# Attention blocks of the first 256 tokens worked by token halves, their FFN in 128-token units, and a written-out order

## The chip, the cores and the metric

The kernel runs on one core of one Trainium2 chip. A core has five engines that run at the same time and wait for each other by semaphores: TensorE (PE, matmuls into PSUM), VectorE (DVE), ScalarE (ACT), GpSimd (POOL) and SyncE (SP, which here only issues transfers). Transfers (DMA) run beside them on 16 DMA engines; they are issued from the queues of SP, ACT and POOL. Each engine takes its instructions strictly in the order in which they were recorded.

The metric is the device time of one execution in microseconds (us). Before the change it is 300.65 us, the median of three runs (299.34 to 301.24).

## What is computed

Sparse attention, followed by a gated FFN on its output, cut to what matters:

```python
B, H, S, D = 4, 8, 768, 64                       # q, k, v, float32
k_min, k_max = min and max of k over chunks of 32 tokens
ub = sum over d of max(q * k_min, q * k_max)     # a bound per query and chunk, causal by chunk
top = the 6 chunks of largest ub                 # per query
scores = q @ k.T / 8, masked to those chunks and to earlier tokens
x = softmax(scores) @ v                          # -> (3072 tokens, 512)
xn = x / sqrt(mean(x * x) + 1e-6) * rms_g
g, val = xn @ w_gate, xn @ w_val                 # 512 -> 1536
out = (g * sigmoid(g) * val) @ w_out             # 1536 -> 512, float32
```

A query in the first 192 tokens has at most 6 chunks before it, so only the last 64 queries of the first 256 tokens need the choice of chunks.

## The kernel before

**Tiling.** The work is twelve blocks of 256 tokens of one batch element, in the order `(0,0) (1,0) (2,0) (3,0) (0,1) (1,1) (0,2) (2,1) (1,2) (3,1) (2,2) (3,2)` (batch element, block). This text counts them from 0. The eight heads are two groups of four. A block's attention needs the keys and values of its own and the earlier blocks of its batch element, so the first four blocks need only themselves. The first half of the FFN, 512 to 1536, is twelve matmul groups for each block, six for gate and six for value; a group fills one PSUM bank (128 x 512).

**One block.** Loads of k, q and v (line 528); `job` transposes k and q in 32 x 32 squares on VectorE (794), casts them to bf16 (`half`, 801 on ScalarE or 802 on GpSimd), takes the minimum and maximum of each chunk (809) and prepares the bounds' operands (815 to 888). `pick` computes the bounds on TensorE (680; 698 for the first four blocks), and on VectorE the six best chunks and from them a mask (723 to 755). `unit` computes scores (922) and adds the mask by a matmul (933); exp (972), a triangle that zeroes later tokens (942, GpSimd), then `values` (998), a reciprocal (1013) and a normalization (1017). `norm` takes the mean square (1034 ScalarE, 1040 and 1042 GpSimd), scales (1052 to 1068) and turns the tokens into `xsT` (on TensorE with an eviction at 1087 or 1091 for the first four blocks, by a DMA transpose for the others). `ffn` does gate and value (1122), tanh (1129), tg (1133), a copy of the value (1141), the product hh (1144 on GpSimd, 1137 on VectorE), the projection (1169), its eviction (1184 or 1187) and the store (1191).

**The first blocks.** Blocks 0 to 2 (`PACKED`) load k and q so that eight tokens lie together in a partition. For blocks 0 and 1 (`SPLIT`) scores, exp and values are done in two parts by tokens, for each head group by itself, xsT by 128 tokens, and the first third of gate and value in groups of sixteen matmuls of 128 columns; all other groups are eight matmuls of 256 columns. For blocks 0 to 2 (`APART`) each head group has its own `pick`. Block 3 loads k and q in sixteen transfers and v in two.

**Order.** `Plan.op` records each operation with its engine or engines, reads, writes and buffers; `Plan.run` (255) then sets the order with a model of costs: it takes, time by time, the operation whose inputs and buffers are there, by a table of due times (`DUE`, 125). Where TensorE would stand idle in the first 60 us of that plan, it puts in matmuls that write nothing of use (1245): narrow ones at first, wide ones later. Two things hold back transfers. `GATES` (508) makes the weights' loads wait for the first `dk` of block 0, and `HELD` (584) makes block 2's loads wait for the second third of wg, and block 3's for the first of wo. Weights come in thirds, in the order wg0, wv0, wg1, wv1, wg2, wv2, wo0, wo1, wo2, issued from GpSimd's queue, which also does work; loads and stores are issued from SP's.

Buffers: kraw 2, qraw 3 and vraw 2 (each a whole block), pt 4, hh 13, rden 3, two pairs of PSUM banks for scores (S) and four banks for the rest (F).

Of the kernel before, what the change touches and what calls it, by code (L numbers as in the profile page):

```python
# [18 lines left out]
HUGE = 3.0e38  # L19


# [15 lines left out]
class Rings:  # L37
    FETCHED = 3.3

    def __init__(self):  # L40
        self.now = 0.0
        self.queue = {}
        self.wait = []

    def _step(self, until):
        while True:
            heads = [q[0] for q in self.queue.values() if q]
            nxt = self.wait[0][0] if self.wait else None
            if not heads:
                if nxt is None or nxt > until:  # L50
                    return
                self.now = max(self.now, nxt)
            else:
                cycle = sum(d[1] for d in heads)
                end = self.now + min(d[0] for d in heads) * cycle
                stop = min(end, until, nxt if nxt is not None else end)
                if stop > self.now:
                    for d in heads:
                        d[0] -= (stop - self.now) / cycle
                    self.now = stop  # L60
                for q in self.queue.values():
                    if q and q[0][0] <= 1e-9:
                        q[0][2](self.now)
                        q.pop(0)
            while self.wait and self.wait[0][0] <= self.now + 1e-12:
                _, ring, d = self.wait.pop(0)
                ahead = sum(x[0] * x[1] for x in self.queue.get("POOL", ()))
                if ring != "POOL" and not d[3] and ahead > 0.0 and not self.queue.get(ring):
                    d[3] = True
                    self.wait.append((self.now + min(self.FETCHED, ahead), ring, d))  # L70
                    self.wait.sort(key=lambda w: w[0])
                    continue
                self.queue.setdefault(ring, []).append(d)
            if self.now >= until and not (self.wait and self.wait[0][0] <= until):
                if not any(q and q[0][0] <= 1e-9 for q in self.queue.values()):
                    return

    def add(self, t, ring, packets, cost, op):
        self._step(min(t, self.wait[0][0]) if self.wait else t)

        def landed(now, op=op):
            op.done = now + (0.9 if op.dma[2] else 1.2) + op.slack
        op.done = None
        self.wait.append((t, ring, [packets, cost, landed, False]))
        self.wait.sort(key=lambda w: w[0])
        self.guess()

    def room(self, ring, t):

        other = Rings()  # L90
        other.now = self.now
        other.queue = {r: [list(d) for d in q] for r, q in self.queue.items()}
        other.wait = [(w, r, list(d)) for w, r, d in self.wait]
        for q in list(other.queue.values()) + [[d for w, r, d in other.wait]]:
            for d in q:
                d[2] = lambda now: None

        def held():
            return sum(d[0] for d in other.queue.get(ring, ())) + sum(
                d[0] for w, r, d in other.wait if r == ring)  # L100

        while held() > 85.0:
            t = max(t, other.now) + 0.25
            other._step(t)
        return t

    def guess(self):
        other = Rings()
        other.now = self.now
        other.queue = {r: [list(d) for d in q] for r, q in self.queue.items()}  # L110
        other.wait = [(t, r, list(d)) for t, r, d in self.wait]
        other._step(1e9)


class Plan:

    SHARES = ("qx", "scale", "relu", "bd0", "bd1", "dk", "mk")
    PATIENT = {"DVE": 0.6, "ACT": 0.6}  # L120
    STICK = 25
    RESERVED = ("hh",)
    HOP = {"PE": 0.055, "ACT": 0.04, "DVE": 0.04, "POOL": 0.075, "SP": 0.06}

    DUE = (
# [282 lines left out]
def kernel(  # L408
# [796 lines left out]
    for i in range(len(ORDER)):  # L1205
# [3 lines left out]
        if i > 1:  # L1209
            loads(i)  # L1210
# [68 lines left out]
```

## Time and profile before

| | us |
|---|---|
| median of three runs (lowest, highest) | 300.65 (299.34, 301.24) |
| span of the profiled execution, first to last instruction | 297.4 |
| busy: TensorE | 282.5 (95% of the span) |
| busy: VectorE | 217.1 (73%) |
| busy: ScalarE | 216.7 (73%) |
| busy: GpSimd | 155.6 (52%) |
| bytes moved by DMA | 35.08 MB, 118 GB/s over the span |

The span is the profiled execution's own time as far as the page gives one; the runs of the table's first line are timed around the whole program. "Busy" counts filler matmuls too. Where the engine named as a bound is busy nearly throughout, the reader looks for the stretches where it is not, and for what of its work is not needed.

### The profile page before, as it was taken

The numbers are of one execution on the slowest core, as the hardware profiler recorded it, in microseconds if no ns is written. First come the engines' busy times: TensorE is split into PE (matmuls) and PEld (weight loads), VectorE is DVE, ScalarE is ACT, GpSimd is POOL, SyncE is SP. The second block draws the span as 40 slices with busy tenths as digits, with TensorE's granted clock in tenths as the row PEclk, the third lists the DMA queues.
The fourth block names the chain that finished last, engine by engine and source line by source line (L and its number), as shares of the span: only waits on it lengthen the run. The fifth ranks groups of instructions, "written<-read, shape, count | busy, mean of one in ns | idle before, by whom it ended". The sixth has DMA issues, their size and how long they took to land.

```text
span 297.4 us, 11418 instructions
## 1 busy us (share of the span) xinstructions
PE 282.5 (95%) x4672; PEld 213.4 (72%) x4672; DVE 217.1 (73%) x623; ACT 216.7 (73%) x372; POOL 155.6 (52%) x266
## 2 busy tenths in 40 slices
PE   7879999999999996999999999899999999999994
PEld 7548777657858854878767787488688778678763
DVE  6987774977998998888999999679356454456430
ACT  4897877688979876987985797677587668565331
POOL 4885858755976864475583276538044114214120
PEclk9999999999999999999999999999999999999998
DMA  7999998755676656654768576511014021011011
GB/s 188 208 204 206 255 197 163 159 130 134 141 194 154 144 136 103 149 100 110 205 135 162 108 193 150 133 40 39 0 57 55 1 82 30 2 73 35 2 71 71
DMA packets 86388, 35.08 MB, mean 118 GB/s; under 512 B 74816, under 2 KB 81728, under 8 KB 86336
## 3 DMA queue, kind: packets, MB, share of 16 engines
q1 hardware_dynamic: 80736, 29.12, 42.6%
q0 software_dynamic: 4752, 4.72, 9.4%
q8 instruction: 36, 0.59, 0.8%
q10 hardware_dynamic: 848, 0.53, 0.7%
q14 instruction: 16, 0.13, 0.2%
HBM read 28.58 MB, written 6.29 MB: 117 GB/s over the span
## 4 chain that ended last, share of the span: by engine, by line
PE 76%; DMA 9%; DVE 4%; ACT 4%; SPq 3%; POOL 1%; issue 1%; DVEq 0%; POOLq 0%; ACTq 0%
PE F L1122 39%; PE F L1169 18%; PE S L922 6%; PE F L998 6%; PE F L680 3%; SPq L528 3%; PE S L933 2%; DMA xsT<-xs 2%; DMA qraw<-in_q_dram 2%; DMA vraw<-in_v_dram 2%; DMA kraw<-in_k_dram 2%; DVE kx L809 1%; POOL hh L1144 1%; DVE m L739 1%; ACT th L1129 1%
## 5 line engine op out<-in xcount | busy, mean ns | idle before, releaser
L972 ACT ACTIVATE pt<-S 128x1024 bf16<-128x1024 f32 (+3 forms) x104 | 85.6, 857 | 19.7 <-PE S L933 18.2
L1144 POOL TENSOR_TENSOR hh<-tg,vs 128x512 bf16<-128x512 bf16 x48 | 55.7, 1164 | 42.6 <-ACT vs L1141 22.9
L1133 DVE SCALAR_TENSOR_TENSOR tg<-th,F 128x512 bf16<-128x512 bf16 x72 | 48.4, 680 | 39.3 <-ACT th L1129 33.7
L1122 PE MATMUL F<-xsT,wg 128*128 128x256 bf16 (+1 forms) x608 | 72.6, 267 | 3.7 <-DVE xnat L1017 1.7
L1122 PE MATMUL F<-xsT,wv 128*128 128x256 bf16 (+1 forms) x608 | 72.4, 267 | 0.6 <-DMA xsT<-xs 0.3
L1169 PE MATMUL F<-wo,hh 128*128 128x512 bf16 (+1 forms) x300 | 68.5, 371 | 1.8 <-POOL hh L1144 0.6
L1122 PEld LDWEIGHTS <-wg 128*128 128x128 bf16 x608 | 55.6, 98 | 13.5 <-issue 2.7
L1122 PEld LDWEIGHTS <-wv 128*128 128x128 bf16 x608 | 55.2, 98 | 9.7 <-DMA vraw<-in_v_dram 0.8
L1129 ACT ACTIVATE th<-F 128x512 bf16<-128x512 f32 x72 | 42.5, 598 | 19.7 <-PE F L1122 17.4
L942 POOL TENSOR_SCALAR_AFFINE_SELECT pt<-pt 128x512 bf16<-128x512 bf16 x48 | 32.2, 674 | 32.3 <-ACT pt L972 31.7
L1169 PEld LDWEIGHTS <-hh 128*128 128x128 bf16 x300 | 27.7, 98 | 28.4 <-issue 1.8
L1141 ACT ACTIVATE vs<-F 128x512 bf16<-128x512 f32 x48 | 28.7, 598 | 13.2 <-PE F L1122 10.1
L922 PE MATMUL S<-qb,kb 32*128 32x256 bf16 (+1 forms) x800 | 32.8, 253 | 2.3 <-ACT qb L801 2.0
L809 DVE TENSOR_REDUCE kx<-kT 128x16 f32<-128x512 f32 x48 | 30.4, 664 | 0.0
L998 PEld LDWEIGHTS <-pt 128*128 128x128 bf16 x672 | 24.8, 98 | 3.1 <-issue 0.3
L998 PE MATMUL F<-VX,pt 128*128 128x65 bf16 x672 | 26.6, 194 | 0.2 <-ACT vs L1141 0.2
L922 PEld LDWEIGHTS <-kb 32*128 32x128 bf16 x800 | 13.9, 92 | 15.0 <-issue 14.4
L933 PE MATMUL S<-mtd,chunkrow 32*128 32x128 bf16 (+2 forms) x384 | 20.5, 203 | 0.2 <-issue 0.2
L933 PE MATMUL S<-mto,chunkrow 32*128 32x128 bf16 (+2 forms) x384 | 19.9, 203 | 0.0
L1017 DVE TENSOR_TENSOR xnat<-F,rden 128x256 bf16<-128x256 f32 x48 | 19.2, 415 | 0.7
L933 PEld LDWEIGHTS <-chunkrow 32*128 32x128 bf16 x768 | 18.5, 93 | 1.2 <-issue 0.4
L1034 ACT ACTIVATE junk<-xnat 128x512 bf16<-128x512 bf16 x24 | 15.1, 631 | 5.4 <-DVE xnat L1017 5.0
(71 smaller groups left out, 337.2 us busy)
## 6 DMA issues: line engine op xcount, KB each, us to landing
vraw<-in_v_dram SPq DMA_DIRECT2D x24, 256.0 KB, 4.4
out_dram<-osb SPq DMA_DIRECT2D x23, 256.0 KB, 2.4
kraw<-in_k_dram SPq DMA_DIRECT2D x72, 64.0 KB, 2.4
qraw<-in_q_dram SPq DMA_DIRECT2D x72, 64.0 KB, 2.2
QX<-qT SPq DMA_DIRECT2D x32, 64.0 KB, 2.7
wg<-in_moe_w_gate_dram POOLq DMA_DIRECT2D x3, 512.0 KB, 12.3
wv<-in_moe_w_val_dram POOLq DMA_DIRECT2D x3, 512.0 KB, 14.3
wo<-in_moe_w_out_dram POOLq DMA_DIRECT2D x3, 512.0 KB, 23.5
```

What stands on the lines that cost most here:

```text
L809: plan.op(f"ext{n}{J}", "DVE", 0.585, 0.67, lambda n=n, op=op: VE.tensor_reduce(out=at(kx)[:, g, n], in_=at(kT).rearrange("p h (j c x) -> ...
L922: TE.matmul(s[a // 2][:, a % 2, c0:c0 + q1 - q0], kbt[r, t, ks], qbt[r, t, q0:q1], start=(t == 0), stop=(t == 1 and not mask), skip_group_ ...
L933: TE.matmul(o, chunkrow[r, BLK * kg + P * e:BLK * kg + P * (e + 1)], mv, start=False, stop=(d == 1), skip_group_check=True)
L942: GE.affine_select(out=d, in_=d, compare_op=ALU.is_ge, fill=0.0, base=0, pattern=[[0, 4], [1, P]], channel_multiplier=-1)
L972: lambda pt=pt, hs=hs, c0=c0, c1=c1, x=sc[hp]: SE.activation(out=at(pt)[:, hs, c0:c1], in_=at(x)[:, :, c0:c1], func=ACT.Exp, scale=SCALE), ...
L998: TE.matmul(o[:, a, :], p_[:, a, off:off + P], vt[:, e, a, :], start=(kb_ == 0 and a == 0), stop=(kb_ == nkb - 1 and a == 3), skip_group_c ...
L1122: TE.matmul(at(p_)[:, n * W:(n + 1) * W], w[:, g, ht * P:(ht + 1) * P], at(xT)[:, g, x0:x0 + W], start=(g == 0), stop=(g == NP - 1), skip_ ...
L1129: plan.op(f"tanh{U}.{hp}", "ACT", 0.48, 0.6, lambda th=th, gp=gp: SE.activation(out=at(th), in_=at(gp), func=ACT.Tanh, scale=0.5), pri - 0 ...
L1133: VE.scalar_tensor_tensor(out=at(tg), in0=at(th), scalar=1.0, in1=at(gp), op0=ALU.add, op1=ALU.mult), pri - 30, reads=[th, gp], writes=[tg ...
L1141: plan.op(f"vcopy{U}.{hp}", "ACT", 0.48, 0.6, lambda vs=vs, vp=vp: SE.activation(out=at(vs), in_=at(vp), func=ACT.Copy), pri + 0.1, reads= ...
L1144: plan.op(f"hh{U}.{hp}", "POOL", 1.11, 1.16, lambda tg=tg, vs=vs, hh=hh: GE.tensor_tensor(out=at(hh), in0=at(tg), in1=at(vs), op=ALU.mult) ...
L1169: TE.matmul(at(op)[:, cs], at(key)[:, o:o + P], wo[:, ht, cs], start=(ht == 0), stop=(ht == NHT - 1), skip_group_check=True)
```

## The change

**Blocks 0 to 3** are now done by `early`, in eight units of 128 tokens, in the order (0,0) (1,0) (0,1) (1,1) (2,0) (2,1) (3,0) (3,1) (block, half). A load brings one unit's k or q of four heads, with four tokens together in a partition, in 128 KB; block 3 is loaded in this way too, with eight transfers for k and q. Buffers for raw data are halved and doubled in number (kraw 4, qraw 6, vraw 4). A unit's transpose, cast, minimum and maximum cover all eight heads. The first half needs no choice of chunks: its scores for both head groups are one operation, with two exp and two triangles of 128 x 512. The second half has one `pick` for both groups, then scores, exp and triangle for each group. Every 128 tokens have an rms, a turn and an xsT of their own.

**Their FFN** is all in groups of sixteen matmuls of 128 columns, a third of gate or value at a time. **Later blocks** do what they did; layouts of kx, BD and VX are changed to suit.

**The order** is no longer planned: `SEQUENCE` lists the operations, `SLOTS` the buffers, `CHOICE` the engine where there are several, `WARM` the fillers (46 narrow, 35 wide; before 77 and 39). `HELD` is empty; `GATES` names the first transpose of k. Where the weights' issues now stand in GpSimd's queue: wg0 and wv0 after the first two triangles; wg1 and wv1 with thirteen operations ahead of them after those; wg2 behind the first hh; wv2 after the next rms; wo0 after the fifth hh, wo1 after the next rms, wo2 after one hh more. The recorded operations number 1553, before 1580, without fillers.

```diff
+SEQUENCE = [
+    3, 34, 35, 36, 37, 25, 19, 13, 6, 21, 23, 33, 29, 44, 0, 30, 7, 17, 16, 1, 22, 18, 14, 39, 26, 27, 40, 45,
...
+WARM = [
+    (42, 46, 0, 0), (63, 8, 0, 1), (89, 11, 2, 1), (102, 5, 0, 1), (111, 2, 1, 1), (119, 4, 2, 1), (181, 2, 2,
+    1), (310, 3, 2, 1)]
...
-    def run(self, in_order=(), fill=None):
+    def run(self, fill):
...
+        self.slot = dict(zip(keys, SLOTS))
...
+        for place, x in enumerate(SEQUENCE):
...
-    buffers("kraw", 2, [P, NG, 8, 2, CH], FP32)
-    buffers("qraw", 3, [P, NG, 8, 2, CH], FP32)
-    buffers("vraw", 2, [P, 2, NG, 4, D], FP32)
+    buffers("kraw", 4, [P, 512], FP32)
+    buffers("qraw", 6, [P, 512], FP32)
+    buffers("vraw", 4, [P, NG, 4, D], FP32)
...
-    buffers("rden", 3, [P, 4], FP32)
+    buffers("rden", 8, [P, 4], FP32)
...
-    GATES = {"0": "dk(0, 0, 0)", "1": "dk(0, 0, 0)", "2": "dk(0, 0, 0)", "o": "dk(0, 0, 0)"}
-    SPLIT = {0, 1}
-    APART = {0, 1, 2}
+    GATES = {x: "turn k(0, 0)" for x in "012o"}
+    EARLY = {0, 1, 2, 3}
+    UNITS = [(0, 0), (1, 0), (0, 1), (1, 1), (2, 0), (2, 1), (3, 0), (3, 1)]
...
-    HELD = {2: (("wg", 1), ("wg", 1)), 3: (("wo", 0), ("wo", 1))}
+    HELD = {}
...
+    def load_early(i, nm, src, x):
+        b, m = ORDER[i]
+        key = (nm + "raw", b, m, x)
+        sv = src[b].rearrange("(g a) (m x r j) d -> g m x a r (j d)", a=4, m=NBLK, x=2, r=32)
+        for g in range(NG):
+            dma(f"load {nm}{b}{m}{x}{g}", ("SP", "ACT")[g] if (i, x) == (0, 0) else "SP", sv[g, m, x],
+                lambda g=g: at(key)[:, 256 * g:256 * (g + 1)], 8, 0.051, -500 + 10 * i + x, writes=[key],
+                takes=() if g else [(key, nm + "raw")], behind=() if g else HELD.get((i, x), ()))
...
+    def early(i):
...
+                def half(eng, T=T, hb=hb):
+                    o, t = flat(hb).rearrange("p (y r j) -> p y j r", j=4, r=32), quads(flat(T))
...
+        prepare(0)
...
+        def first():
+            for g in range(NG):
+                product([at(x)[:, :, P * g:P * (g + 1)] for x in sc], kcols(b, 0, g, 0), qcols(0, g), False)
...
+        yield
+        prepare(1)
...
+        pick(i, tuple(range(NG)))
...
+            def second(g=g, sc=sc):
+                for e in range(2):
+                    s = [at(x)[:, :, P * e:P * (e + 1)] for x in sc]
+                    product(s, kcols(b, 0, g, e), qcols(1, g), True)
+                    forbid(s, mtd, mto, g, P * e, slice(0, 1))
...
-    def ffn(i):
-        cut = NHT // 3 if i in SPLIT else 0
-        pieces = [((s,), h) for s in whole for h in range(0, cut, 4)] + [
-            (whole, h) for h in range(cut, NHT, 2)]
+    def ffn(i, pieces):
...
+    units = {i: early(i) for i in sorted(EARLY)}
+    for i, x in UNITS:
+        next(units[i], None)
+        norm(i, (x,), due_attn(i) + (7 if x else -3))
...
+    thirds = range(0, NHT, NHT // 3)
+    for h in thirds:
+        for i, x in UNITS[:4]:
+            ffn(i, [((x,), h)])
+    for i, x in UNITS[:4]:
+        project_out(i, (x,))
+    for i, x in UNITS[4:]:
+        ffn(i, [((x,), h) for h in thirds])
+        project_out(i, (x,))
+    for i in range(len(ORDER)):
+        if i not in EARLY:
+            ffn(i, [((0, 1), h) for h in range(0, NHT, 2)])
+            project_out(i, (0, 1))
```

The order of the first operations of TensorE after the change: scores of unit (0, 0), of (1, 0), values of both, turn (0, 0), pick 0, first gate group of (0, 0), turn (1, 0), pick 1, first second-half scores of block 0, first gate group of (1, 0), and from there FFN groups of blocks 0 and 1 with the second halves' attention between them; the first projection follows after the last of the 24 groups of blocks 0 and 1.

More of the change, by code (lines that the diff above doesn't have):

```diff
@@ L34, in __init__ @@
         self.alts = {eng: (occ, lat, fn)}
[L37 to L112, printed above, removed]
@@ L392, in run @@
             for key in o.uses:
[L393 removed]
                 left[key] -= 1
                 if not left[key]:
[L396 removed]
+                    held[self.pool_of[key], self.slot[key]] = None
+            gone.add(x)
             order.append(o)
[L398 to L401 removed]
         self.order = order
[L403 removed]
@@ new lines, in job @@
+            o = plan.op(f"scores{J}{kg}", "PE", pe, pe + 0.2, unit, pri,
+                        reads=keys(b, kg, g) + [qb, mtd, mto, mtd + (g,), mto + (g,), "chunkrow"],
+                        writes=sc + [pt], takes=[(x, "S") for x in sc] + [(pt, "pt")])
+            o.mode = "row"
+            for hp in range(2):
+                hs = slice(2 * hp, 2 * hp + 2)
+                plan.op(f"exp{J}{kg}{hp}", "ACT", occ, lat, lambda pt=pt, hs=hs, c1=c1, x=sc[hp]: SE.activation(
+                    out=at(pt)[:, hs, 0:c1], in_=at(x)[:, :, 0:c1], func=ACT.Exp, scale=SCALE), pri,
+                    reads=[sc[hp], pt], writes=[pt + (hp,)])
+                if kg == m:
+                    plan.op(f"tri{J}{hp}", "POOL", 0.595, 0.64, triangle(pt, hs, BLK, 0), pri,
+                            reads=[pt + (hp,), pt], writes=[pt + ("t", hp)])
```

737 lines of the change are left out of this document (328 added, 409 removed), and 198 rows, old and new, of tables (DUE, SEQUENCE, SLOTS).

## The prediction

> **What bounds the kernel now.** The page comes first: which engine is full, and in which slices it isn't.
>
> ```profile
> PE 282.5 (95%) x4672; PEld 213.4 (72%) x4672; DVE 217.1 (73%) x623; ACT 216.7 (73%) x372; POOL 155.6 (52%) x266
> ...
> PE   7879999999999996999999999899999999999994
> ```
>
> TensorE is the bound: 282.5 of 297.4 us, so 14.9 us idle, and the gaps lie in the first slices, in the one of 6 tenths (about 112 to 119 us) and at the end. But part of the busy time is filler. The groups kept apart by shape:
>
> ```profile
> L1245 PE MATMUL F<-chunkrow,ident 128*128 128x512 bf16 x39 | 10.2, 380 | 0.0
> ...
> L1245 PE MATMUL F<-ident 128*128 128x128 bf16 x77 | 6.4, 265 | 1.7 <-POOL eps L551 1.7
> ```
>
> Line 1245 writes nothing that is used. The small ones take 6.4 us in one run; the wide ones, at the 0.22 us a piece that ten 128x512 projections show below (2.32 us with the last drain), 8.5. Idle and filler make 29.8 us, useful matmuls some 267.6. No order can win more than those 29.8. Where they lie, the timeline of TensorE tells (start, duration, what):
>
> ```profile
> 22.85 1.07 PE L1122 MATMUL F<-xsT,wg 128*128 128x128 bf16 x16
> ...
> 41.99 1.07 PE L1122 MATMUL F<-xsT,wg 128*128 128x128 bf16 x16
> 42.89 1.06 PE L1122 MATMUL F<-xsT,wv 128*128 128x128 bf16 x16
> ...
> 49.56 2.32 PE L1169 MATMUL F<-wo,hh 128*128 128x512 bf16 x10
> ...
> 55.33 1.04 PE L1122 MATMUL F<-xsT,wg 128*128 128x256 bf16 x8
> ...
> 58.09 1.04 PE L1122 MATMUL F<-xsT,wg 128*128 128x256 bf16 x8
> 58.97 1.04 PE L1122 MATMUL F<-xsT,wv 128*128 128x256 bf16 x8
> 59.93 0.43 PE L698 MATMUL F<-qT,BO 64*64 64x32 f32 x16
> ...
> 60.65 0.42 PE L698 MATMUL F<-qraw,BO 64*64 64x32 f32 x16
> ```
>
> The reader should see that the first FFN matmul stands at 22.85 us; that before it TensorE has only the small attention of two blocks; and that the FFN of the first two blocks, 24 groups of 0.88 us (58.09 to 58.97) or 21 us, is through only at 59.85. Two thirds of the loss are start-up. The start-up waits for data. Bytes moved and shares of the DMA engines by stretch (last two columns: DMA share, GB/s):
>
> ```profile
> 0.00:5.00 5.00, 3.29 (x32) 3.29 (x33) 2.84 (x4) 1.49 (x2) 3.61 (x34) 1.00 0.61 161
> 5.00:10.00 5.00, 3.94 (x59) 3.43 (x58) 4.60 (x8) 4.08 (x5) 1.58 (x6) 1.00 1.09 224
> 10.00:15.00 5.00, 5.00 (x126) 2.89 (x124) 4.34 (x24) 4.09 (x11) 5.00 (x8) 1.00 1.09 210
> ```
>
> From 5 us on the DMA engines are full. And the weights, by tile (issue times on POOL, then time to landing):
>
> ```profile
> L528 POOL DMA_DIRECT2D wg<-in_moe_w_gate_dram x3: 767/777/992, 9.8 to 14.2; - x3
> DMA to landing us min/median/max: 7.9/12.3/17.8
> L528 POOL DMA_DIRECT2D wv<-in_moe_w_val_dram x3: 773/775/777, 10.8 to 15.0; - x3
> DMA to landing us min/median/max: 10.2/14.3/21.6
> L528 POOL DMA_DIRECT2D wo<-in_moe_w_out_dram x3: 747/762/857, 16.4 to 21.8; - x3
> DMA to landing us min/median/max: 22.6/23.5/25.2
> ```
>
> So the first third of wg lands at 17.7, of wv at 21.0, the last of wg at 32.0, of wv at 36.6, wo from 39 to 47: about 3.4 to 4.5 us apart.
>
> **The change part by part.** *FFN of the first four blocks in 128-token units.* Before, 8 groups were of sixteen 128-column matmuls; now 48 are. 41.99 to 42.89 is 0.90 us for sixteen, against 0.88 for eight of 256: forty groups more at 0.02 is 0.8 us at most, and I take 0.3. The weight loads double there (640 more); the row below gives 98 ns for one, so if none were hidden sixteen would take 1.57 us and the forty groups 27 us more. They are hidden in the two groups above, so zero is the end I take.
>
> ```profile
> L1122 PEld LDWEIGHTS <-wg 128*128 128x128 bf16 x608 | 55.6, 98 | 13.5 <-issue 2.7
> ```
>
> The Trainium skill (TensorE: Matmul & The Clock Gate, Back-to-back issue gap) speaks against this part: a sustained stream of weight load and matmul takes about 81 ns each at 128 columns, not the 56 of an isolated one. By it the 640 small matmuls that replace 320 wide ones would cost an estimated 16 us. The two groups above, at 56 ns, do not agree with it.
>
> *The first unit sooner.* Work now starts when half a block has landed, 128 tokens of all heads. Two rows show how landing follows bytes:
>
> ```profile
> 5.07 1.30 DVE L794 STREAM_TRANSPOSE kT<-kraw 128x512 f32<-128x512 f32 x2 [0.54 <-DMA kraw<-in_k_dram]
> ...
> 17.06 0.71 DVE L794 STREAM_TRANSPOSE qT<-qraw 128x512 f32<-128x512 f32 x1 [0.60 <-DMA qraw<-in_q_dram]
> ```
>
> The first 0.5 MB is usable at 5.07, and 2.6 MB (k, q, v of block 0, k, q of block 1) at 17.06, with the weights beside them from 9.8 on. In the new order of SP the first 0.5 MB are k and q of the first 128 tokens. So the first scores and values come sooner. But VectorE's queue then holds the transpose of the second half of block 1's k ahead of the reciprocals of unit (1, 0), and ScalarE's holds that unit's square ahead of the first xsT. That k is the 2.4th MB. Without the weights it would land at 13.4 (2.4 MB by the three rates, plus 1.2), with them by 17.0: I take 15, in the middle. From there, at these means:
>
> ```profile
> L809 DVE TENSOR_REDUCE kx<-kT 128x16 f32<-128x512 f32 x48 | 30.4, 664 | 0.0
> L1017 DVE TENSOR_TENSOR xnat<-F,rden 128x256 bf16<-128x256 f32 x48 | 19.2, 415 | 0.7
> L794 DVE STREAM_TRANSPOSE kT<-kraw 128x512 f32<-128x512 f32 x24 | 16.1, 692 | 1.2 <-DMA kraw<-in_k_dram 1.1
> ...
> L1034 ACT ACTIVATE junk<-xnat 128x512 bf16<-128x512 bf16 x24 | 15.1, 631 | 5.4 <-DVE xnat L1017 5.0
> ...
> L1087 ACT ACTIVATE xsT<-F,rmsg 128x128 bf16<-128x128 bf16 x8 | 2.3, 395 | 0.0
> ```
>
> transpose 0.7, reciprocals 0.3, one reduction 0.7, two norms 0.8, square 0.8, four xsT activations 1.2: first FFN group at 19.4, 3.4 us sooner than 22.85. The first wg is there (17.7).
>
> *Picks of both head groups at once.* Twelve of them instead of fifteen on VectorE; its rows are small and it idles in this stage. In the sum: nothing.
>
> *Weights later, and behind work.* The issues of the first third stay near 9.8. But POOL now has small work between the others: thirteen operations, two rms among them, stand ahead of the second third's two (I get 15.5 and 21 us), and ahead of the last third two triangles, two casts of k and q, a cast of v and one hh:
>
> ```profile
> L1144 POOL TENSOR_TENSOR hh<-tg,vs 128x512 bf16<-128x512 bf16 x48 | 55.7, 1164 | 42.6 <-ACT vs L1141 22.9 <-DVE tg L1133 18.7 <-DVE mtd L749 1.0
> ...
> L942 POOL TENSOR_SCALAR_AFFINE_SELECT pt<-pt 128x512 bf16<-128x512 bf16 x48 | 32.2, 674 | 32.3 <-ACT pt L972 31.7
> ```
>
> That hh needs the gate and value groups of unit (1, 0), done by my count at 26; so the last wg goes out at about 28.8 (it was 14.2). It lands 7.9 us later at the most favourable row, less if the queue is empty; I take 35.5, and wv at 39.2. Queued behind wg is the rms of unit (0, 1), whose xsT TensorE takes up at about 32: just in time.
>
> *TensorE's queue, added up.* After 19.4: the picks keep the second group to 23; four groups of the first third to 26.1; with the second third at 25.5 and 29, units (0, 0), (1, 0) and (0, 1) and the second scores to 34.7; the last third at 35.5: three gate groups to 38.2, wait to 39.2, then ten groups (8.8), a turn (0.2), one pick of matmuls (1.1, as 59.93 to 61.1) and one unit of scores (0.5): 49.9. All 24 groups are then done, with the same attention as before at 49.56, where 20 were (the last four stand at 55.33 to 59.85). Lead: 4 x 0.88 less 0.35, or 3.2 us.
>
> *What is late next.* The last wo, behind an hh of the last third on POOL, lands at about 50.4 (four weights 3.7 apart after 39.2 would say 50.3), and the first projection waits 0.5 for it. On SP the loads of block (1, 1)'s k stand ahead of block 2's v and wait for a k buffer that the transpose of block 3 frees; that stands behind a tg of unit (1, 1), whose group TensorE does at 43 to 44 in the count above, so at about 46. That v then lands at 53 to 54, and the values of block 2 wait some 0.4. In exchange the guards of block 2's and 3's loads on weights are gone, and block 3's load comes in 10 pieces and not 18:
>
> ```profile
> 40.02 9.24 SPq L528 DMA_DIRECT2D kraw<-in_k_dram  x8
> ```
>
> Lead after this: 2.3, less 0.3 for the 128-column groups, 2.0.
>
> *The rest, in a new order.* From 60 us on the same operations follow in another order. Before, TensorE's stalls there are few; the largest two in the chain of waits of 38 to 292 us:
>
> ```profile
> PE F L1122 <- DVE xnat L1017: 1.7, 1, 1.7
> PE F L1122 <- ACT xsT L1087: 0.7, 1, 0.7
> ```
>
> All of them come to 5.7 us, and the first is block 4's FFN waiting for its attention. Bounds: 5.7 us gained to about as much lost, since a new order can stall as often. The loads of blocks (0, 1) and (1, 1) are now issued some 10 us sooner, so I take the 1.7 stall as mostly gone: 1.3 gained.
>
> Sum: 2.0 + 1.3 = 3.3 us, span 294.1. The page gives 297.4 for the span, the median is 300.65; the 3.25 us around it I leave as they are: **297.3 us**. A difference of 1%, 3 us, is about what a measurement of this kernel can tell.
>
> **The rivals.**
> *More than that* (291 to 295.5): the first FFN and the last weights come as soon as the favourable bounds allow (k at 13.4, the last wg at 34), 2 to 3 us more, and the middle stalls go. For it: ScalarE has work taken away (nine casts and copies fewer, two evictions of outputs more). Against it: TensorE needs the last third anyway.
> *Nothing gained* (299 to 302.5): a lead of 2 to 3 us is lost in the middle, where VectorE is nearly as full as TensorE:
>
> ```profile
> 160.00:170.00 10.00, 10.00 (x180) 6.54 (x163) 9.76 (x51) 6.95 (x13) 3.00 (x7) 1.00 0.72 118
> ```
>
> Or TensorE runs slow at the start. There are 46 small fillers instead of 77, and the trace shows their pace rising only after some 4 us, though the granted clock reads 1.00:
>
> ```profile
> 3.00:4.00 1.00, 1.00 (x12) 1.00 (x11) 1.00 (x1) 0.99 (x2) 1.00 (x7) 1.00 1.14 309
> 7.00:8.00 1.00, 1.00 (x20) 0.92 (x17) 0.73 (x2) 0.91 (x1) 0.00 (x0) 1.00 1.30 223
> ```
>
> At 12 per us instead of 20, the four FFN groups of 19 to 26 us would take 2 us more.
> *Slower: the last weights come too late* (302.5 to 307). Place: POOL's issues behind hh. If the last third goes out after 34 and not 28.8, because vs, tg and hh slip with the chain before them, the last wo lands at 56, and TensorE, whose queue is fixed, stands there with no other FFN. Break-even is the last wo at about 53.6; each us beyond costs one, and late v of block 2 adds to it. For it: POOL idles 42.6 us ahead of hh already now. Against it: before, the last wo landed at 47 with less urgency.
> *Slower by the 128-column groups* (308 and more: a third of the 27 us above, and up), if weight loads do not hide in long runs.
>
> **How the numbers follow.** Forecast (295.5 to 299) 0.38; more 0.20; nothing 0.21; late weights 0.17; weight loads 0.04. Faster by over 1% (below 297.6) takes the second and three quarters of the first: 0.48. Slower by over 1% (above 303.7): most of the last two: 0.19; between: 0.33. The range 291.5 to 303.5 leaves out the last case, two thirds of late weights and the far end of more, some 0.2.
>
> **What would show it.** Right: first FFN at 18 to 20.5 us; last wg landed near 35.5; all 24 groups before the first projection, at 49 to 52; sixteen 128-column matmuls in 0.9 us throughout; the stall near 115 gone. Wrong: the first projection after 53, a VectorE share above 95% with TensorE gaps between 80 and 190, or FFN groups of 1.3 us.

## The result, and the profile after

The changed kernel takes 338.04 us (median of four runs, 337.17 to 338.52) beside 300.43 us for the kernel before on the same chip: a ratio of 1.123 (95% interval 1.119 to 1.128). It is 37.6 us slower. The forecast was 297.3 us with a range of 291.5 to 303.5, so both sign and range were wrong. Here and below a ratio compares undisturbed executions of a kernel with those of the kernel before on the same chip, so it need not be the quotient of two medians. The profiled execution took 338.44 us, with a span of 336.7.

The page of the changed kernel answers to the first lines of the prediction. Its third line is TensorE in 40 slices of 8.4 us, then come the granted clock, the DMA engines and the rate:

```profile
PE 293.0 (87%) x4989; PEld 224.0 (67%) x4989; DVE 219.4 (65%) x617; ACT 209.2 (62%) x365; POOL 160.3 (48%) x263
...
PE   5462988428869999998999989999999999999995
...
PEclk9577699959969999997999999999999999999999
DMA  1395929941665556857646487832120200202102
GB/s 60 119 187 111 188 53 145 187 93 33 163 167 114 127 127 157 183 138 104 152 90 157 118 204 153 173 81 66 22 77 3 64 2 33 64 3 62 66 33 95
```

The reader should see three things. TensorE's idle time has grown from 14.9 to 43.7 us (336.7 less 293.0), and most of it lies in the first twelve slices, 100 us. Its clock falls there too. And the DMA engines, full from 5 us on before, stand at 1 and 3 tenths in the first two slices, while the other engines are mostly idle. The stretches say it more finely (last two columns: DMA share and GB/s):

```profile
0.00:5.00 5.00, 3.58 (x34) 3.58 (x35) 1.39 (x2) 1.49 (x2) 1.73 (x22) 1.00 0.12 35
5.00:10.00 5.00, 1.11 (x15) 1.02 (x13) 1.00 (x2) 0.00 (x0) 1.63 (x4) 0.90 0.27 96
10.00:15.00 5.00, 3.15 (x23) 1.28 (x23) 2.27 (x4) 2.42 (x3) 0.88 (x1) 0.50 0.44 135
15.00:20.00 5.00, 1.23 (x16) 0.44 (x17) 2.42 (x5) 1.67 (x2) 3.58 (x10) 0.84 0.67 143
```

Before, the first three of these read 161, 224 and 210 GB/s at shares of 0.61, 1.09 and 1.09. Now 5 to 10 us has 96 GB/s at a share of 0.27, though loads are queued throughout. A share of 0.27 is 4.3 of 16 engines. VectorE's timeline shows the data coming late (start, duration, what; in brackets the idle time before and what ended it):

```profile
6.49 0.71 DVE L668 STREAM_TRANSPOSE kT<-kraw 128x512 f32<-128x512 f32 x1 [3.66 <-DMA kraw<-in_k_dram]
...
28.91 0.71 DVE L668 STREAM_TRANSPOSE QX<-qraw 128x512 f32<-128x512 f32 x1 [6.48 <-DMA qraw<-in_q_dram]
...
32.04 0.71 DVE L668 STREAM_TRANSPOSE kT<-kraw 128x512 f32<-128x512 f32 x1 [2.42 <-DMA vraw<-in_v_dram]
...
72.65 0.71 DVE L668 STREAM_TRANSPOSE QX<-qraw 128x512 f32<-128x512 f32 x1 [11.61 <-DMA qraw<-in_q_dram]
```

The row at 32.04 is k of unit (1, 1), which the prediction had landed at 15, and the one at 72.65 is q of unit (2, 1). On TensorE the first FFN group follows that k, behind four filler matmuls (L1177), and the first projection stands at 84.42 us (49.56 before):

```profile
35.88 1.89 PE L1177 MATMUL F<-chunkrow,ident 128*128 128x512 bf16 x4
37.56 1.91 PE L1038 MATMUL F<-xsT,wg 128*128 128x128 bf16 x16
...
52.72 1.05 PE L1038 MATMUL F<-xsT,wg 128*128 128x128 bf16 x16
53.61 1.06 PE L1038 MATMUL F<-xsT,wv 128*128 128x128 bf16 x16
54.50 1.06 PE L1038 MATMUL F<-xsT,wg 128*128 128x128 bf16 x16
...
55.65 2.84 PE L1038 MATMUL F<-xsT,wg 128*128 128x128 bf16 x48
...
74.00 1.86 PE L1038 MATMUL F<-xsT,wg 128*128 128x128 bf16 x16 [11.32 <-DVE xsT L1011]
```

There are two separate losses: a late first group (37.56 against 22.85) and a stall of 11.3 us ahead of 74.00, for an xsT on VectorE. VectorE itself waited 11.6 us for q, at 72.65. That q stood on SP behind k of block 3, which waited for a k buffer. SP's own queue:

```profile
2.32 4.80 SPq L349 DMA_DIRECT2D kraw<-in_k_dram  x4
...
32.72 21.47 SPq L349 DMA_DIRECT2D kraw<-in_k_dram  x6
...
61.28 23.31 SPq L349 DMA_DIRECT2D kraw<-in_k_dram  x6
84.68 0.40 SPq L349 DMA_DIRECT2D vraw<-in_v_dram  x1
```

Four issues take 4.80 us, 1.2 us each (before, the four of k at 5.21 us took 2.77, 0.69 each), and twice the queue stands for over 20 us. In the first of these rows k of block 3 waits until VectorE has transposed k of block 2, at 52.92.

### The profile page after: what moved, and what is told of

It reads as the page before. It is cut to its first block, busy times and chain, and to the rows that moved or that the text cites. A ratio compares the mean times of both kernels' runs of the same rounds, so it can differ in the third digit from the quotient of the medians.

```text
span 336.7 us, 11993 instructions
## 1 busy us (share of the span) xinstructions
PE 293.0 (87%) x4989; PEld 224.0 (67%) x4989; DVE 219.4 (65%) x617; ACT 209.2 (62%) x365; POOL 160.3 (48%) x263
## 2 busy tenths in 40 slices
DMA packets 84343, 35.13 MB, mean 104 GB/s; under 512 B 70208, under 2 KB 81216, under 8 KB 84288
## 4 chain that ended last, share of the span: by engine, by line
PE 49%; DMA 13%; SPq 12%; DVE 11%; ACT 5%; issue 5%; POOL 5%; DVEq 0%; ACTq 0%; POOLq 0%
PE F L1038 23%; PE F L1088 13%; SPq L349 11%; DMA qraw<-in_q_dram 7%; PE F L625 4%; PE S L604 4%; DVE tg L1049 2%; DMA vraw<-in_v_dram 2%; DVE xs L972 2%; POOL hh L1060 2%; DMA QX<-qT 2%; PE S L615 2%; PE F L493 1%; PE F L506 1%; ACT junk L954 1%
## 5 line engine op out<-in xcount | busy, mean ns | idle before, releaser
L1038 PE MATMUL F<-xsT,wg 128*128 128x128 bf16 (+1 forms) x768 | 75.1, 251 | 11.6 <-DVE xsT L1011 11.3
L928 ACT ACTIVATE pt<-S 128x1024 bf16<-128x1024 f32 (+1 forms) x80 | 71.6, 940 | 21.4 <-PE S L615 21.0
L1038 PE MATMUL F<-xsT,wv 128*128 128x128 bf16 (+1 forms) x768 | 74.3, 249 | 2.9 <-DVE tg L1049 1.5
L1038 PEld LDWEIGHTS <-wg 128*128 128x128 bf16 x768 | 60.8, 100 | 20.0 <-issue 12.6
L1088 PE MATMUL F<-wo,hh 128*128 128x512 bf16 (+1 forms) x300 | 70.0, 376 | 0.6 <-DVE osb L1106 0.6
L1038 PEld LDWEIGHTS <-wv 128*128 128x128 bf16 x768 | 59.8, 99 | 10.5 <-issue 1.9
L1057 ACT ACTIVATE vs<-F 128x512 bf16<-128x512 f32 x48 | 28.4, 602 | 19.5 <-PE F L1038 15.5
L604 PEld LDWEIGHTS <-kb 32*128 32x128 bf16 x832 | 14.7, 93 | 23.2 <-issue 18.5
L625 PE MATMUL F<-VX,pt 128*128 128x65 bf16 x672 | 27.8, 195 | 0.9 <-POOL VX L581 0.7
L588 POOL TENSOR_SCALAR_AFFINE_SELECT pt<-pt 128x512 bf16<-128x512 bf16 x32 | 21.3, 678 | 15.3 <-ACT pt L928 15.1
L836 DVE TENSOR_REDUCE kx<-kT 128x16 f32<-128x512 f32 x32 | 21.2, 668 | 0.1
```

Source lines behind the costliest of these rows:

```text
L588: GE.affine_select(out=d, in_=d, compare_op=ALU.is_ge, fill=0.0, base=0, pattern=[[0, 4], [1, P]], channel_multiplier=-1)
L604: TE.matmul(s[a // 2][:, a % 2, :], k_[r, t, :], q_[r, t, :], start=(t == 0), stop=(t == 1 and not mask), skip_group_check=True)
L625: TE.matmul(o[:, a, :], w_(a), at(vx)[:, g, a, :], start=(n == 0 and a == 0), stop=(n == nkb - 1 and a == 3), skip_group_check=True)
L928: plan.op(f"exp{J}{kg}{hp}", "ACT", occ, lat, lambda pt=pt, hs=hs, c1=c1, x=sc[hp]: SE.activation(out=at(pt)[:, hs, 0:c1], in_=at(x)[:, :, ...
L1038: TE.matmul(at(p_)[:, n * W:(n + 1) * W], w[:, g, ht * P:(ht + 1) * P], at(xT)[:, g, x0:x0 + W], start=(g == 0), stop=(g == NP - 1), skip_ ...
L1057: plan.op(f"vcopy{U}.{hp}", "ACT", 0.48, 0.6, lambda vs=vs, vp=vp: SE.activation(out=at(vs), in_=at(vp), func=ACT.Copy), pri + 0.1, reads= ...
```

## The experiments

**The theory.** `load_early` takes the source as `(g a) (m x r j) d -> g m x a r (j d)`: four heads (`a`) are slowest, then 32 rows. The loads it replaces had one head and 32 rows slowest. If the slowest dimension says on how many DMA engines a transfer is spread, the new ones use 4 of 16, and the share of 0.27 is explained. The rivals: SP's new order and its waits for k buffers hold the loads, whatever a transfer takes; TensorE's slow clock costs the time; the new order of work is itself worse.

**1. Spread the loads.** The same bytes, buffers and order, other transfers:

```diff
-sv = src[b].rearrange("(g a) (m x r j) d -> g m x a r (j d)", ...)      # 128 KB: 4 heads x 32 rows x 1 KB
+sv = src[b].rearrange("(g a) (m x r j) d -> a m x r g (j d)", ...)      # 64 KB: 32 rows x 2 groups x 1 KB
...
+for c in (2 * n, 2 * n + 1):                                            # two transfers for one
+    dma_start(out=at(key)[32 * c:32 * (c + 1)].rearrange("p (g f) -> p g f", g=NG), in_=sv[c, m, x])
```

> The changed kernel, with each early load of k and q of 128 KB (four heads slowest, 1 KB pieces, into 128 partitions) cut the other way: two transfers of 64 KB, each one head of both groups into 32 partitions, again in 1 KB pieces. Same bytes, buffers, order and waits; twice as many issues on SP. Theory 1 (a transfer whose slowest dimension is 4 is spread over 4 of the 16 DMA engines; the changed kernel's DMA share is 0.27 and its rate 95 to 98 GB/s from 4 to 10 us, against 1.09 and 224 GB/s before): DMA share above 0.8 and about 200 GB/s from 5 to 10 us, first FFN group at 19 to 25 us instead of 37.6, time 295 to 303 us. Theory 2 (the order of SP's queue and the four k buffers hold the loads, whatever a transfer takes): first FFN group still after 33, time 330 to 340. Theory 3 (the slow TensorE clock of the start costs the time): a few us less only, 325 to 335.

Measured: 317.16 us, ratio 1.049 (1.043 to 1.056). By the ratios 7.4 of the 12.3% are gone, and the rival of the clock alone (325 to 335) and that of order and buffers (330 to 340) are out as the main cause. But the forecast of this step, 295 to 303, was missed too. Its stretches, from 5 to 20 us:

```profile
5.00:10.00 5.00, 3.79 (x38) 2.46 (x37) 2.52 (x4) 2.43 (x3) 3.51 (x11) 1.00 0.55 144
10.00:15.00 5.00, 2.67 (x34) 1.53 (x34) 4.30 (x11) 4.13 (x6) 3.14 (x6) 1.00 0.95 179
15.00:20.00 5.00, 1.96 (x15) 0.77 (x14) 0.71 (x1) 1.14 (x4) 1.63 (x4) 1.00 1.18 212
```

The rate is 144 GB/s, not 200: SP now issues eight transfers of 64 KB in 3.62 us, 0.45 us each, and 64 KB in 0.45 us is 145 GB/s. The first FFN group stands at 27.66.

**2. Put the same pattern into the kernel before.** Only its packed loads are changed, four transfers of 128 KB as they were:

```diff
-sv = src[b].rearrange("(g a) (m r j) d -> a m r g (j d)", a=4, m=NBLK, r=32)[a, m]
+sv = src[b].rearrange("(g a) (m r s j) d -> g m s a r (j d)", a=4, m=NBLK, r=32, s=2)[g, m, s]
```

> The kernel before, with the packed k and q loads of its first three blocks (four transfers of 128 KB, one head of both groups each, 32 rows slowest, 2 KB pieces) cut by head group and tokens instead: again four of 128 KB, but four heads slowest and 1 KB pieces, into 128 partitions, as the changed kernel has them. Everything else is as before. Theory 1 (4 of 16 DMA engines): DMA share about 0.3 and some 100 GB/s in the first 10 us, 1.5 MB of k and q of blocks 0 and 1 take 16 us and not 7, the first FFN group stands 8 to 15 us later than 22.85, time 308 to 320 us. Theory 2 (order and buffers of the new kernel): 300 to 303 us.

Measured: 328.61 us, ratio 1.090 (1.085 to 1.096), worse than expected. Its first two stretches, and its first FFN group, at 44.48 instead of 22.85:

```profile
0.00:5.00 5.00, 3.29 (x36) 3.29 (x37) 2.83 (x4) 0.00 (x0) 3.36 (x33) 1.00 0.11 28
5.00:10.00 5.00, 2.46 (x45) 2.29 (x41) 0.50 (x1) 1.49 (x2) 0.10 (x1) 1.00 0.44 135
```

```profile
44.48 1.89 PE L1123 MATMUL F<-xsT,wg 128*128 128x128 bf16 x16
```

The DMA share is 0.28 and the rate 82 GB/s over these 10 us, near the 0.3 and 100 expected; the loads of v, whose pattern is as before, are among them from 6 us on. (The k and q of blocks 0 and 1 are 2 MB, sixteen transfers of 128 KB, and not the 1.5 MB of the expectation, which at some 100 GB/s take 21 us instead of the 16 it names.) Nothing of the new order is in this kernel, so the pattern, smaller pieces included, costs the kernel before 9%.

**3. The control for it:** the kernel before with 64 KB transfers of 1 KB pieces, 32 rows slowest.

```diff
-sv = src[b].rearrange("(g a) (m r j) d -> a m r g (j d)", ...)[a, m]          # one transfer of 128 KB
+sv = src[b].rearrange("(g a) (m r s j) d -> a m s r g (j d)", ..., s=2)       # two of 64 KB: sv[a, m, 0], sv[a, m, 1]
```

> The kernel before with each packed load of k and q of 128 KB cut by tokens into two of 64 KB with 1 KB pieces; 32 rows stay slowest, so all DMA engines carry it. The control for the kernel whose packed loads have four heads slowest (328.61 us), with its piece size and more issues. If the count of issues and the piece size matter (0.45 us of SP for 64 KB), 302 to 306 us with the first FFN group 2 to 4 us later than 22.85; if only the spread matters, 299.5 to 302 us.

Measured: 308.98 us, ratio 1.031 (1.027 to 1.034). More transfers for the same bytes cost 9 us, more than the 302 to 306 expected; the first FFN group stands at 27.66, 4.8 us later than before. So of the 9.0% of experiment 2, 3.1% comes with piece size and count (this control has twice the issues, so that share is if anything too large), and the other 6% with what is slowest.

**4. Two heads slowest.** This parts the slowest dimension from the size and number of the transfers, which are those of experiment 1:

```diff
-sv = src[b].rearrange("(g a) (m x r j) d -> a m x r g (j d)", ...)       # 32 rows slowest, 64 KB
+sv = src[b].rearrange("(g c a) (m x r j) d -> g c m x a r (j d)", c=2, a=2, ...)   # 2 heads slowest, 64 KB
```

> The changed kernel, with each early load of k and q cut by heads into two transfers of 64 KB: two heads slowest, 1 KB pieces, into 64 partitions. Number, size and piece size of the transfers are those of the kernel with spread loads (317.16 us); only what is slowest differs, 2 instead of 32. If the slowest dimension sets how many DMA engines carry a transfer: 2 of 16, a DMA share of 0.13 to 0.25 and 50 to 95 GB/s from 4 to 10 us, and a time well above the 338.04 us of four heads slowest, 350 to 390 us. If instead the size or the 128 partitions of the destination made the changed kernel's loads slow: 317 to 338 us.

Measured: 377.45 us, ratio 1.253 (1.245 to 1.261), as expected. From 5 to 25 us its stretches are all alike in DMA share and rate; the first and the last of the four:

```profile
5.00:10.00 5.00, 0.59 (x11) 0.42 (x8) 0.00 (x0) 0.68 (x2) 0.00 (x0) 0.79 0.14 48
...
20.00:25.00 5.00, 1.72 (x5) 0.34 (x3) 1.28 (x2) 0.00 (x0) 1.20 (x3) 0.84 0.14 48
```

Two heads: share 0.14, 48 GB/s. Four heads: 0.27, 96 GB/s. Both give 24 GB/s for one of the slowest dimension, so the slowest dimension sets the rate. The number of partitions written does not: with 128, 64 and 32 of them (changed kernel, this one, experiment 1) the rates are 96, 48 and 144 GB/s. The Trainium skill (DMA: Bandwidth & Descriptors, Why a DMA increments its semaphore by 16 and not by 1) says this beforehand: the transfer goes to the largest number of engines up to 16 that divides the slowest dimension of source and destination, and a transfer issued from SP or ScalarE takes the lowest-numbered ones, so loads on different queues share the same few. The shares of 0.14 and 0.27, of 16 engines 2.2 and 4.3, agree with it. Which engines they were, and that queues share them, no run here shows.

**5. Which loads cost it.** Blocks 0 and 1 spread, blocks 2 and 3 left with four heads slowest:

```diff
+        if i > 1:
+            ...                      # load_early as in the changed kernel
+            return
+        ...                          # load_early of experiment 1
```

> The changed kernel with the loads of blocks 0 and 1 alone spread over all DMA engines; those of blocks 2 and 3 keep four heads slowest. If the loss of the form lies in the start alone, 317 to 320 us, as with all of them spread; if the later loads, behind which SP's queue stands, cost as much, 325 to 330 us.

Measured: 326.15 us, ratio 1.088 (1.084 to 1.092). Spreading the start's loads wins 3.5% (1.123 to 1.088), spreading those of blocks 2 and 3 another 3.9% (to 1.049). About half of what spreading wins, a third of the whole loss, thus lies behind the start. The first FFN group stands at 27.55, as with all loads spread, but the second stall is 9.18 us:

```profile
61.67 1.87 PE L1050 MATMUL F<-xsT,wg 128*128 128x128 bf16 x16 [9.18 <-DVE xsT L1023]
```

With all loads spread it is 4.57. From 60 to 100 us TensorE is busy for 32.66 us here and for 39.52 there: SP's queue stands, as above, and what is behind it lands later still.

**6. The order on SP.** Experiment 1 still has the second stall, 4.57 us on TensorE for xsT ahead of 56.38. VectorE's row shows for what:

```profile
55.04 0.71 DVE L673 STREAM_TRANSPOSE QX<-qraw 128x512 f32<-128x512 f32 x1 [4.86 <-DMA qraw<-in_q_dram]
55.67 0.65 DVE L1016 TENSOR_TENSOR xsT<-F,rmsg 128x512 bf16<-128x512 bf16 x1
```

The q is that of unit (2, 1), and its load stands on SP behind k of block 3, which needs a k buffer. So:

```diff
 SP: ... k(2, 0) k(2, 1)
+    q(2, 0) q(2, 1)
     k(3, 1) k(3, 0)
-    q(2, 0)
     k of block (0, 1), ...
-    q(2, 1) ...
```

> The kernel with spread early loads (317.16 us), and in SP's queue the four loads of q of block 2 set ahead of the k loads of block 3, which wait for a k buffer. Their own buffers are free from the start. Theory A (what is left of the loss after the loads are spread is in part a stall at 50 to 55 us: VectorE's queue holds the xsT of unit (1, 1) behind the transpose of q of unit (2, 1), whose load stands on SP behind a k load that waits from 22.6 to 43.7 us): VectorE's 4.9 us wait for q and TensorE's 4.6 us wait for xsT go, TensorE's clock does not fall at 56 us; 308 to 314 us. Theory B (the stall is hidden by later work): within 2 us of 317.

Measured: 314.46 us, ratio 1.037 (1.025 to 1.049). The stall is gone (TensorE is busy for 5.00 of 5.00 us from 50 to 55, 1.81 in experiment 1), and the time is just above the 308 to 314 expected of it; but the interval overlaps that of experiment 1, so the size of the gain is not settled.

**7. Two queues.** Eight of the early transfers issued by ScalarE, without and with the edit of experiment 6:

```diff
-"SP"
+"ACT" if (i, x, nm) in ((1, 0, "q"), (1, 1, "k")) else "SP"
...
-named["table"].after += [o for o in plan.ops if o.dma and o.eng == "ACT"]   # ScalarE's first table load no longer waits for all its transfers
```

> The kernel with spread early loads (317.16 us), and the loads of q of unit (1, 0) and k of unit (1, 1), eight transfers of 64 KB, issued from ScalarE's queue instead of SP's. Theory A (SP's issue rate, a 64 KB transfer each 0.45 us or about 145 GB/s, now holds the loads: DMA share 0.55 from 5 to 10 us): DMA share above 0.8 from 5 to 10 us, k of (1, 1) usable some 4 us before 22.0, the first FFN group at 23 to 25 us instead of 27.7, 312 to 315 us. Theory B (the weights beside them decide): first FFN group and time within 1 us of the kernel compared.

> The two edits together: q of block 2 ahead of k of block 3 on SP, and eight early transfers on ScalarE's queue. If both hold and add, 304 to 310 us; if the second only uncovers a wait for weights or for block 2, within 2 us of the first alone.

Measured: 314.26 us, 1.040 (1.031 to 1.050), and together 311.51 us, 1.035 (1.028 to 1.041). The first is within its 312 to 315. The second is in neither of the ranges named for it (304 to 310, or within 2 us of 314.46 or 314.26). The two together are faster than experiment 1, but neither edit is told apart from the two together. The first FFN group comes at 24.34 and 24.65, as expected, but the DMA share from 5 to 10 us is 0.68 and 0.57, not 0.8. In the second kernel, while both queues issue, each transfer takes some 0.62 us of its queue (ScalarE's q below: six in 3.70). And ScalarE then stands behind its second pair of loads for 4.6 us:

```profile
1.72 3.70 ACTq L350 DMA_DIRECT2D qraw<-in_q_dram  x6
...
11.41 2.87 ACTq L350 DMA_DIRECT2D kraw<-in_k_dram  x2
14.33 1.34 ACT L682 ACTIVATE qb<-qT 128x512 bf16<-128x512 f32 x1 [4.58 <-DMA kraw<-in_k_dram]
```

**8. The clock.** Experiment 1 with more filler in its two gaps:

```diff
-(102, 5, 0, 1), ...
+(102, 18, 0, 1), ..., (253, 18, 1, 1), ...
```

> The kernel with spread early loads (317.16 us), with 13 more wide filler matmuls ahead of the first turn of tokens and 18 ahead of the value group at 50.75 us, in two gaps of TensorE (17.6 to 21.8 and 51.8 to 56.4 us). Nothing else changed. Theory C (the granted clock falls to about a half after TensorE has stood idle for some microseconds, as at 20 to 25 us, 0.60, and 55 to 60 us, 0.51, and the FFN groups behind the gaps run at 1.7 to 1.9 us instead of 0.9 per sixteen): clock near 1.0 in both stretches, 313 to 315.5 us. Theory D (the clock does not matter, or falls anyway): 316.5 to 319 us.

Measured: 318.76 us, ratio 1.050 (1.037 to 1.063): no gain is shown, though the interval could hide one of 1%. The filler did its work: the clock reads 1.00 in every stretch up to 70 us, and the first projection stands at 62.88 instead of 66.54. Of these 3.7 us only 1.2 are left at the end of the profiled executions (spans of 316.7 and 317.9). In between TensorE waited for GpSimd, and its clock fell to 0.50 at 74 to 78 us (see the last section). What the slow clock alone costs stays open, since it came back in another place.

**9. The order with late loads left out.** Experiment 6 without some of the early loads of k and q, first those of units (0, 1) and (1, 1), then all but those of the first two units:

```diff
-in_=[sv[c, m, x] for c in (2 * n, 2 * n + 1)]
+in_=[sv[c, m, x] for c in (2 * n, 2 * n + 1)] if (i, x) not in ((0, 1), (1, 1)) else []   # first kernel
+in_=[sv[c, m, x] for c in (2 * n, 2 * n + 1)] if i < 2 and x == 0 else []                # second kernel
```

> The kernel with spread early loads and q of block 2 ahead of k of block 3 (314.46 us), with the k and q loads of units (0, 1) and (1, 1) left out: 0.5 MB, sixteen transfers of 64 KB on SP. Their transposes read the raw data of units (0, 0) and (1, 0) instead, so the attention of the second half of blocks 0 and 1 is computed from the wrong tokens. It asks what the new order is worth when these loads are not late. Theory A (the order is sound, what is left of the loss is late loads): first FFN group at 17 to 20 us, 295 to 302 us. Theory B (the order itself stalls TensorE, after the start too): first FFN group as early, but 303 to 309 us, with the stalls behind 60 us still there.

> As the kernel without the k and q loads of units (0, 1) and (1, 1) (304.22 us), with those of blocks 2 and 3 left out too: another 1 MB, 32 transfers. All early transposes but those of units (0, 0) and (1, 0) read the raw data of unit (0, 0) or (1, 0), so the attention of the other six units is computed from the wrong tokens. If the rest of the loss still is late loads and SP's waits for k buffers behind them: 297 to 301 us. If it is the new order's own waits: 302 to 305 us.

Measured: 304.22 us, 1.015 (1.011 to 1.019), and 304.25 us, 1.011 (1.003 to 1.018). Both are in the ranges named for an order that has waits of its own (303 to 309, 302 to 305). The expectations miscount the bytes: sixteen transfers of 64 KB are 1 MB (the page has 34.08 MB moved instead of 35.13), and with 32 more 3 MB are left out. Even with these 3 MB of loads spared, which the kernel before has to make, the new order does not beat it. The second kernel's first FFN group stands at 19.70 us and its first projection at 51.91. Now ScalarE and VectorE are what is full in the start; two stretches of the second kernel:

```profile
10.00:15.00 5.00, 3.85 (x45) 2.09 (x45) 4.03 (x13) 5.00 (x9) 4.07 (x9) 1.00 0.97 162
15.00:20.00 5.00, 4.00 (x84) 2.17 (x83) 4.93 (x22) 3.43 (x9) 4.57 (x12) 1.00 1.22 196
```

ScalarE is busy for 5.00 of 5.00 us, then VectorE for 4.93. The early casts to bf16 (`half`) are part of it. The groups by shape of the second kernel, a later block's cast and then an early one (busy time, mean ns of one), and under them four early casts of the kernel before, in two rows of ScalarE's timeline:

```profile
L835 ACT ACTIVATE qb<-qT 128x512 bf16<-128x512 f32 x8 | 5.1, 639 | 0.0
...
L685 ACT ACTIVATE qb<-qT 128x512 bf16<-128x512 f32 x2 | 2.7, 1344 | 2.0 <-DVE qT L675 2.0
```

```profile
5.81 2.10 ACT L801 ACTIVATE kb<-kT 128x512 bf16<-128x512 f32 x2 [1.63 <-DVE kT L794]
8.01 2.07 ACT L801 ACTIVATE qb<-qT 128x512 bf16<-128x512 f32 x2
```

An early cast on ScalarE takes 1.34 us now, some 1.04 before, and 0.64 in the later blocks. Whether this is what keeps the order from winning was not tried.

## Why the prediction was wrong

*What failed* first is one term, the landing of k of unit (1, 1): "That k is the 2.4th MB", "I take 15", with bounds of 13.4 and 17.0. The bounds were worked out from 161, 224 and 210 GB/s, which are the rates of the loads that the change removes. The new loads have another shape, and no row of the trace showed that shape; the step should have asked on how many engines it is spread. That k was transposed at 32.04. No rival had this mechanism. The "slower" rival, late weights, put a price of some 5 us on another place. The second failure is a wait on SP that the sum leaves out (below). The first projection came at 84.42, 34.0 us behind the 50.4 of the prediction's count: 18.2 of these are there at the first group, 11.3 are the second stall, and the other 4.5 were not followed up.

*The first FFN group at 19.4.* It came at 37.56. The chain behind that k was about right: from its transpose at 32.04 to the end of the four xsT activations it takes 3.95 us, where the terms add up to 4.5 and 4.4 was counted.

```profile
34.87 1.12 ACT L1007 ACTIVATE xsT<-F,rmsg 128x128 bf16<-128x128 bf16 x4
```

What the chain left out is TensorE's own queue: the four fillers at 35.88, 1.89 us at a granted clock of 0.53 (35 to 40 us), stand ahead of the group. In the two kernels of experiment 9, where k of unit (1, 1) is not loaded, its transpose stands at 13.40 and 13.51 and the first group at 18.73 and 19.70. That these are near 19.4 is luck, since the forecast was for a k that lands.

*128-column groups, 0.3 us.* Right. At full clock groups start 0.89 us apart (52.72, 53.61, 54.50), and 48 matmuls take 2.84 us with their drain: the additional weight loads are hidden. (They are 320, not the 640 of the prediction: LDWEIGHTS of wg and wv are 768 each, before 608.) The Trainium skill's 81 ns (TensorE: Matmul & The Clock Gate, Back-to-back issue gap) would make an estimated 3.9 us of those 48, which the trace again does not agree with.

*Weights behind POOL's work.* The mechanism was right and the times were not, since the chain before them slipped:

```profile
30.86 0.86 POOL L349 DMA_DIRECT2D wg<-in_moe_w_gate_dram  x1
...
37.03 0.86 POOL L349 DMA_DIRECT2D wv<-in_moe_w_val_dram  x1
...
48.94 0.81 POOL L349 DMA_DIRECT2D wg<-in_moe_w_gate_dram  x1
```

15.5, 21 and 28.8 were predicted. Yet no group of matmuls in the first 100 us waits for weights in the changed kernel. Such waits appear in other kernels: 0.96 and 0.67 us with both edits of experiment 7, 0.82 us ahead of the first group in the second kernel of experiment 9, and 2.00 us in that of experiment 4.

*What is late next on SP.* The mechanism was named, k of a later block waiting for a buffer that a transpose frees, but for one of its two places: k of block (1, 1) ahead of block 2's v, the row at 61.28 above, priced at 0.4 us. The place before it, k of block 3 in the row at 32.72, has no term. Behind it stood q of unit (2, 1), and behind that q's transpose, in VectorE's queue, the xsT of unit (1, 1) that TensorE needs. The price was 11.3 us in the changed kernel and 4.6 with the loads spread, and the stall went when experiment 6 moved that q ahead. The prediction followed the queue of SP to one load (v) and did not follow the other (q) into the queue of the engine that uses it.

*The order, 2.0 us of lead and 1.3 later.* This can be read from the second kernel of experiment 9: 24 groups are through before 51.91, where the kernel before needs 49.56 and four groups more (3.5), 53.1. So the lead is 1.2 us, not 2.7 at that point, with data that was sooner than assumed. Later, in two rows of the kernel before and then three of that kernel (after the stretch and its length: TensorE's busy time):

```profile
60.00:100.00 40.00, 38.77 (x636) 28.96 (x636) 35.39 (x120) 35.36 (x67) 27.08 (x40) 1.00 0.62 152
100.00:200.00 100.00, 95.81 (x1875) 72.11 (x1877) 88.17 (x287) 78.58 (x129) 56.22 (x90) 1.00 0.59 133
```

```profile
53.00:60.00 7.00, 5.81 (x100) 2.96 (x98) 5.22 (x11) 3.51 (x7) 5.42 (x10) 1.00 0.73 174
60.00:100.00 40.00, 39.92 (x825) 32.30 (x828) 37.19 (x126) 32.01 (x67) 29.94 (x47) 1.00 0.59 143
100.00:200.00 100.00, 95.86 (x1889) 72.42 (x1882) 91.84 (x284) 76.60 (x126) 54.30 (x84) 1.00 0.62 133
```

TensorE is idle for 5.4 us from 60 to 200 before and 4.2 there: 1.2 gained, near the 1.3 of the forecast, but by luck. The forecast's gain was the stall near 115, and behind 100 us nothing is gained (4.19 and 4.14 idle; 1.79 us go at 119.27 for an xsT). And 1.2 us are lost just ahead, from 53 to 60. The profiled execution of that kernel took 300.16 us; its span of 298.5 is 1.1 us longer than that of the kernel before, and TensorE idles for 17.3 us in it, before for 14.9. By the ratio of 1.011 the order without these loads is slower by 1%, the rival "nothing gained" at best.

*The sum.* By the ratios, of 12.3% lost: 3.5% and 3.9% are four heads slowest in blocks 0 and 1 and in blocks 2 and 3; some 1.2% the order of q and k on SP (not well separated); 2.2% go when k and q of units (0, 1) and (1, 1), 1 MB, are not loaded at all; 0.4% when those of blocks 2 and 3 are not (not separated from zero); and 1.1% (0.3 to 1.8) are left for the order itself. Its cause is open: ScalarE and VectorE are full at its start, and that this is the reason was only argued.

*The time around the span.* 3.25 us was the median less the span of one execution. The changed kernel's profiled execution has 1.7 us around it (338.44 less 336.7), so that the forecast was some 1.5 us too high in this term; it decided nothing.

## What to carry to other kernels

A byte rate belongs to the shape of the transfers that it was read from: when a change rewrites a load's access pattern, look at the slowest dimension of both sides first, and read the DMA share, which at 4 of 16 engines stands flat at 0.27 with loads queued. Keep that dimension wide (32 served here, 4 and 2 did not), and transfers large: here a 64 KB one cost SP 0.45 us, which alone holds the rate to 145 GB/s. And follow a wait on one in-order queue through every load behind it into the queue of the engine that uses it; the dear one was two queues away.

## What the runs showed that was not expected

A transfer on few DMA engines also holds the engine that issues it: SP needed 1.2 us for one of 128 KB on four engines (4.80 for four), and 0.69 us before, where it was spread; 1.7 us for one of 64 KB on two (13.89 for eight), and 0.45 us where it was spread.

The clock can fall after short gaps. In experiment 8, which filled the first gaps, these rows of TensorE stand at 69 to 78 us; ten matmuls of 512 columns took 2.32 us at 62.88:

```profile
62.88 2.32 PE L1091 MATMUL F<-wo,hh 128*128 128x512 bf16 x10
...
69.53 0.67 PE L628 MATMUL F<-VX,pt 128*128 128x65 bf16 x16 [0.78 <-POOL VX L584]
70.05 0.59 PE L1091 MATMUL F<-wo,hh 128*128 128x512 bf16 x2
72.34 0.53 PE L607 MATMUL S<-qb,kb 32*128 32x128 bf16 x16 [1.70 <-POOL qb L683]
...
75.63 4.14 PE L1091 MATMUL F<-wo,hh 128*128 128x512 bf16 x10
```

The granted clock is 1.00 up to 72 us, 0.62 from 72 to 74 and 0.50 from 74 to 78. The Trainium skill (TensorE: Matmul & The Clock Gate, What's actually happening) puts the fall after an idle window of about 3.4 us; here a gap of 1.70 us, with one of 0.78 shortly before it, was enough.
